# First product of expert slot 0 in the last dense block, a new order up to slot 5, and a shared copy of the last slot

## The chip, the cores and the metric

The kernel runs on one core of a Trainium2 chip. The metric is the device time of one execution in microseconds (us); lower is better. The core has engines that run side by side, each with its own queue of instructions taken in order: TensorE (PE; its weight loads are listed as PEld), VectorE (DVE), ScalarE (ACT), GpSimd (POOL) and SyncE (SP), which issues most DMAs. All times below are counted from the first instruction of the profiled execution, unless they are said to be counted from elsewhere.

## The reference

Three stages over 4608 tokens of width 512, cut to what is computed:

```python
# 1. attention in chunks of 64 tokens, 8 heads of 64
attn = softmax(q_c @ k_c.T / 8); out = attn @ v_c
# 2. dense layer, 512 -> 2048 -> 512
h = x @ w_in
g = max(h, 0) + alpha * min(h, 0)
x = g @ w_out
# 3. mixture of 8 experts, each token to its best one, 512 -> 1024 -> 512
logits = x @ w_gate;  expert = argmax(logits)
out[mask] = p[mask] * (max(x[mask] @ w1[e], 0) @ w2[e])   # p: softmax weight of the chosen expert
```

## The kernel before

**Stages.** Tokens are worked in 18 groups of 256, that is 36 tiles of 128 (`NTILE`). For each group attention gives x, and the dense layer takes 16 steps: step (j, m) makes 128 of the 2048 hidden columns (`mm1`, 12 products of 256 columns), and adds what they give to the group's output (`mm2`, 6 products of 512 columns, issued three steps later and interleaved with a later `mm1`). The written loop over steps 32 to 287 has two tables of extra work, `pre` and `bg`: what `at(step, f, ...)` puts there is issued in that step, `bg` behind the step's own `g_a`. The last block, steps 272 to 287, is group 17; `B0` is 272. All products are split in a high and a low part (hi and lo), so 4 slices of the contraction make 12 products.

**Gate and table.** When both tiles of a group are done, `gate_ev` copies a tile's rows out of PSUM on ScalarE, `gate_l` makes the 8 gate products on VectorE, `gate_a` and `gate_e` the choice and the exponential, `gate_r` ranks the tokens with two small products on TensorE (the second uses `ohsum`, the running count), and `gate_b` brings `ohsum` up to date on VectorE and scatters the rows into the expert-sorted buffer `xs` with an indirect DMA on GpSimd. After the last tile (35), `table_count`, `table_experts`, `table_places` and `table_base` compute on VectorE where each slot of 128 sorted rows begins (the register table `rt`).

**Slots.** Expert work goes in slots of 128 rows; 39 are always done here. `load(t)` brings a slot's rows. The first four slots (`FULL`) belong to the expert that has most tokens after group 16, known early; their loads need only that (`first`, `early_pick`). From slot 4 on `load` needs `rt`. `tx(t)` transposes the rows (`blocks`: transpose on VectorE into one of two z buffers, hi copy on ScalarE, lo on GpSimd). `m1(t, f)`, f = 0 or 1, is a first product (12 products of 512 columns) and 16 small copies with a Relu into `hx`, four for each 32-row part I; they run on ScalarE for f = 0 and for slots 0 to 2, otherwise on VectorE (line 728). `th(t, f)` transposes `hx` into `hT` by `blocks` again, `m2(t, f)` is a second product, and for f = 1 the scaling on ScalarE and the scatter to the output on GpSimd. So a slot is four groups of 12 products: (t, 0) and (t, 1) first, then `m2(t, 0)` and `m2(t, 1)`.

**Weights.** They lie split in HBM (`wsp`). The expert ring takes over the dense weights' memory: `load_early(x, c)` brings quarter c of the x-th early expert (2 MB) as soon as the dense layer has read the quarter under it for the last time: `load_early(0, 0..3)` at B0+4, 7, 12 and 15, `load_early(1, 0..3)` in the order below. `m1(t, f)` reads quarter f, `m2(t, f)` quarter 2 + f. Later experts come by `refill`.

**Order.** All is issued in the order in which it is written (`manual_schedule`), each engine takes its part in that order, and only data and buffers make it wait. After the last dense step come `mm2` of the last three steps and then the list `START` (line 920), which holds the last two tiles' gate, the table and the slots up to the second product of slot 4; then the loop of line 986 for the slots from 5 on, with slot t + 1's first products ahead of slot t's second ones.

Of the kernel before, what the change touches and what calls it, by code (L numbers as in the profile page):

```python
# [11 lines left out]
ACTF = mybir.ActivationFunctionType  # L12
ALU = mybir.AluOpType
# [24 lines left out]
def tile_attention_moe(ctx, tc, q, k, v, w_in, w_out, alpha, w_gate, w1, w2, out):  # L38
    nc = tc.nc
    NB = q.shape[0]  # L40
    NTILE = 2 * NB
    FULL = (NTILE - 4) // 8
    NT = 128 * NTILE
    MF = 16
    E = 8
# [57 lines left out]
    def bank(tag, name):  # L103
        return ps.tile([128, 512], F32, tag=tag, name=name)
# [3 lines left out]
    def pair(tag, name):  # L108
        return ps.tile([128, 2, 512], F32, tag=tag, name=name)

    def hbank(name, n=2):
        turn[0] = (turn[0] + 1) % n
        return bank(f"h{turn[0]}", name) if turn[0] < 2 else pair("s", name)[:, 0]
# [264 lines left out]
    def g_b(j, m):  # L378
        g_h(j, m)
        g_l(j, m)  # L380
# [62 lines left out]
        oh, se, lg = ohs[i]  # L443
        nc.scalar.activation(out=lg, in_=lg, func=ACTF.Exp, accum_out=se)

    rks = {}

    def gate_r(i):
        oh = ohs[i][0]
        if i < NTILE - 2:  # L450
            rk = pair("o", "rk")[:, 0, 0:E]
        else:
            rk = bank("y1", "rk")[:, 0:E]
        nc.tensor.matmul(out=rk, lhsT=tri, rhs=oh, start=True, stop=False)
        nc.tensor.matmul(out=rk, lhsT=ones, rhs=ohsum, start=False, stop=True)
        rks[i] = rk
# [114 lines left out]
    def at(step, f, *args):  # L571
        bg.setdefault(step, []).append((f, args))
# [45 lines left out]
    V = nc.vector  # L618
# [44 lines left out]
    xg, gi, xT, hx, hT, yp = {}, {}, {}, {}, {}, {}  # L663
# [32 lines left out]
    def blocks(dst, src):  # L696
        z = sg_u([128, 4, 4, 32], "z")
        V.transpose(out=z.rearrange("p b i r -> p i b r"), in_=src.rearrange("p i (b c) -> p i b c", b=4))  # L698
        z = z.rearrange("p b i r -> p b (i r)")
        nc.scalar.activation(out=dst[:, 0], in_=z, func=ACTF.Copy)  # L700
        nc.gpsimd.tensor_tensor(out=dst[:, 1], in0=z, in1=dst[:, 0].bitcast(F32), op=ALU.subtract)  # L701
# [5 lines left out]
    def passes(out, lhs, c, t, first, last):  # L707
        w = W2[c]
        rows_ = slice(0, 1) if t < FULL else bass.ds(half[t], 1)
        ins = []  # L710
        for a in range(4):
            for n, (xl, wl) in enumerate(((0, 0), (0, 1), (1, 0))):
                ins.append(nc.tensor.matmul(  # L713
                    out=out, lhsT=lhs[:, xl, a], rhs=w[:, rows_, wl, a],
                    start=(first and a == 0 and n == 0), stop=(last and a == 3 and n == 2),
                ))
        marks[t, c] = ins

    def m1(t, f):
        if f == 0 and t >= FULL:  # L720
            half[t] = nc.tensor.value_load(rt[0:1, 5, t:t + 1], min_val=0, max_val=1)
        p = hbank("h", 3)
        passes(p, xT[t], f, t, True, True)
        hx[t, f] = P2["hx"].tile([128, 4, 128], F32, name="hx")
        for I in range(4):
            for J in range(4):
                src, dst = p[32 * I:32 * I + 32, 128 * J:128 * J + 128], hx[t, f][32 * J:32 * J + 32, I]
                if f == 0 or t < FULL - 1:
                    nc.scalar.activation(out=dst, in_=src, func=ACTF.Relu)  # L729
                else:  # L730
                    V.tensor_scalar(out=dst, in0=src, scalar1=0.0, scalar2=None, op0=ALU.max)  # L731

    def th(t, f):
        if f == 0:
            hT[t] = xt_p.tile([128, 2, 2, 4, 128], F32R, tag="xt", name="hT")
        blocks(hT[t][:, f], hx.pop((t, f)))
# [29 lines left out]
        nc.gpsimd.memset(tbl([32, 5, 2, 32], "cols"), 0.0)  # L766

    def table_count():
        cps = pair("o", "cps")[:, 0, 0:E]
        nc.tensor.matmul(out=cps, lhsT=ones, rhs=ohsum, start=True, stop=False)  # L770
        nc.tensor.matmul(out=cps, lhsT=ones, rhs=ohs[NTILE - 1][0], start=False, stop=True)
        n = tbl([128, E], "n")
        V.tensor_tensor(out=n, in0=cps, in1=ebase, op=ALU.subtract)
# [137 lines left out]
    B0 = NS - MF  # L911
    at(B0 + 1, open_p2)
    for t in range(3):
        at(B0 + 2, load, t)
    at(B0 + 2, table_clear)
    at(B0 + 6, tx, 0)
    at(B0 + 6, load, 3)
    at(B0 + 9, tx, 1)
    a, b = NTILE - 2, NTILE - 1
    START = (  # L920
        (mm2, NB - 1, MF - 1), (gate_ev, a), (gate_l, a, 0, 4), (gate_ev, b), (gate_l, a, 4, 8), (gate_l, b, 0, 1),
        (gate_a, a), (m1, 0, 0), (m1, 0, 1), (th, 0, 0), (gate_e, a), (tx, 2), (gate_l, b, 1, 4), (gate_l, b, 4, 8),
        (m1, 1, 0), (load_early, 1, 0), (gate_r, a), (gate_b, a), (gate_a, b), (th, 0, 1), (m1, 1, 1), (tx, 3),
        (m2, 0, 0), (load_early, 1, 1), (gate_r, b), (th, 1, 0), (table_count,), (table_experts,), (gate_e, b),
        (m1, 2, 0), (gate_b, b), (th, 1, 1), (m2, 0, 1), (load_early, 1, 2), (table_places,), (m1, 2, 1),
        (load_early, 1, 3), (table_base,), (th, 2, 0), (table_next,), (th, 2, 1), (load, 4),
        (tx, 4), (m1, 3, 0), (table_refill,), (m2, 1, 0), (m1, 3, 1), (m2, 1, 1), (load, 5), (m2, 2, 0), (th, 3, 0),
        (tx, 5), (m2, 2, 1), (load, 6), (th, 3, 1), (m1, 4, 0), (m1, 4, 1), (tx, 6), (th, 4, 0),
        (m2, 3, 0), (th, 4, 1), (load, 7), (m1, 5, 0),
        (m2, 3, 1), (th, 5, 0), (m1, 5, 1), (refill, 4, 0), (load, 8), (m2, 4, 0), (th, 5, 1), (m2, 4, 1),  # L930
    )
    FIRST = 5

# [4 lines left out]
    with tc.manual_schedule():  # L938
        def warm(n):
            b = bank("h1", "warm")  # L940
            for _ in range(n):
                nc.tensor.matmul(out=b[:, 0:128], lhsT=ident, rhs=ident, start=True, stop=True)

        def by_step(f):
            return lambda x, *e: f(*order[x], *e)

        def hook(d):
            return lambda x: hooks(d, x)

        ops = dict(  # L950
            Q=load_part_qk, I=iload, G=lambda _: load_wgb(), V=load_v, N=lambda _: nc.sync.dma_start(out=calpha, in_=alpha), K=load_qk,
            Z=lambda _: consts(), W=warm, S=at_s, A=soft_a, B=soft_b, E=soft_e, C=soft_c, D=soft_d, T=at_pt, P=at_ptc, O=at_pv, H=at_xh, L=at_xl,
            v=conv_v, s=conv_s, u=conv_u, m=conv_m, h=conv_h, l=conv_l,
            X=by_step(mm1), Y=by_step(mm2), r=by_step(g_r), x=by_step(g_x), f=by_step(g_h), g=by_step(g_l),
            p=hook(pre), b=hook(bg),
        )
        engs = dict(V=nc.vector, G=nc.gpsimd)
        for t in ORDER.split():
            e = t[-1:]
            if e in engs:  # L960
                ops[t[0]](int(t[1:-1]), engs[e])
            else:
                ops[t[0]](int(t[1:]))
        done = 30
        for s in range(32, NS):
            j, m = order[s]
            hooks(pre, s)
            g_b(*order[s - 1])
            if done <= s - 3 and order[done][1]:
                mm1(j, m, mm2_parts(*order[done]))  # L970
                done += 1
            else:
                mm1(j, m)
            g_a(j, m)
            hooks(bg, s)
            while done <= s - 3:
                mm2(*order[done])
                done += 1
        hooks(pre, NS)
        hooks(bg, NS)  # L980
        g_b(j, m)
        mm2(j, m - 2)
        mm2(j, m - 1)
        for f, *args in START:
            f(*args)
        for t in range(FIRST, TS):
            more, two, dyn = t + 1 < TS, t + 2 < TS, t >= FULL
            if two: tx(t + 2)
            if more: m1(t + 1, 0)
            if more: m1(t + 1, 1)  # L990
            if dyn: refill(t, 0)
            if more:
                th(t + 1, 0)
                th(t + 1, 1)
            m2(t, 0)
            m2(t, 1)
            if t > FULL: refill(t - 1, 1)
            if t + 4 < TS: load(t + 4)
        refill(TS - 1, 1)
        n_s = nc.values_load(rt[0:1, 7, 0:1], min_val=NTILE, max_val=T)  # L1000
        with tc.If(n_s > TS):
            for t in range(TS, T):
                with tc.If(n_s > t):
                    load(t)
                    tx(t)
                    for f in range(2):
                        m1(t, f)
                    for f in range(2):
                        th(t, f)
                    for f in range(2):  # L1010
                        m2(t, f)
                    if t + 1 < T:
                        for c in range(2):
                            refill(t, c)
# [43 lines left out]
```

## Time and profile before

| | before |
|---|---|
| median of 3 runs | 1337.11 us (1336.64 to 1337.33) |
| profiled execution | 1337.11 us |
| its span, first to last instruction | 1335.3 us |
| PE busy | 1314.2 us, 98% |
| DVE busy | 971.0 us, 73% |
| ACT busy | 737.2 us, 55% |
| POOL busy | 694.7 us, 52% |
| mean granted TensorE clock | 0.995 of full |

Busy time is that of the engine's own instructions; waiting, and the issue of DMAs, is not counted. Ends of matmuls are modelled, and pipelined ones overlap, so the distance from one matmul's start to the next is the better measure of its cost. In a timeline a row is one or several like instructions in a row: start, time until the last one's end, engine, line, operation, tiles and shapes, count, and in brackets the idle time of the engine before it and what ended it. L12 is line 12 of the kernel. SPq and POOLq are the sequencers that issue DMAs.

### The profile page before, as it was taken

To read this page: it belongs to the slowest core of one execution; us is meant where nothing else is said; L and a number is where in the kernel's file an instruction comes from. 1 tells how busy PE (TensorE), PEld (TensorE's weight loads), DVE (VectorE), ACT (ScalarE), POOL (GpSimd) and SP (SyncE) were. 2 spreads that over 40 slices of the span, in tenths; PEclk is the share of its full clock that TensorE was granted. 3 is DMA by queue.
4 is the path that set the end of the run, shared out by engine and by line. 5 is a ranking of instruction groups with operands and counts; after the bars stand their busy time and mean duration, and the time that the engine had idled before them with its cause. 6 is when DMAs were issued, how large, how long until landed. Compare 5 with 4: busy or idle time off the path is not lost. (4 is left out here: it accounts for less than half of the span.)

```text
span 1335.3 us, 29880 instructions
## 1 busy us (share of the span) xinstructions
PE 1314.2 (98%) x9561; PEld 1146.6 (86%) x9561; DVE 971.0 (73%) x2483; ACT 737.2 (55%) x1961; POOL 694.7 (52%) x726
## 2 busy tenths in 40 slices
PE   8999999999999999999999999999999999999997
PEld 7898889888898888988889888887888888888885
DVE  7987887877877787887887786667766666656653
ACT  5654454555545556455555554338666666666663
POOL 3322346667676675766767664334444444444442
PEclk9999999999999999999999999998999999999999
DMA  9264415666666666566666661295224426866570
GB/s 364 82 202 148 106 49 180 221 201 202 218 208 209 209 213 222 196 225 204 199 221 204 208 213 64 62 338 208 62 59 174 174 62 260 320 248 229 191 272 35
DMA packets 107872, 249.07 MB, mean 187 GB/s; under 512 B 15104, under 2 KB 36096, under 8 KB 102592
## 3 DMA queue, kind: packets, MB, share of 16 engines
q1 hardware_dynamic: 101712, 227.37, 50.6%
q0 software_dynamic: 6000, 19.70, 4.0%
q8 instruction: 84, 1.38, 0.4%
q14 instruction: 76, 0.62, 0.2%
HBM read 401.39 MB, written 88.91 MB: 367 GB/s over the span
## 5 line engine op out<-in xcount | busy, mean ns | idle before, releaser
L342 PEld LDWEIGHTS h<-xt,ring 128*128 128x128 f32 x3456 | 610.3, 188 | 66.6 <-DVE xt L329 1.1
L342 PE MATMUL h<-xt,ring 128*128 128x256 f32 x3456 | 651.9, 282 | 1.0 <-DVE xt L329 0.9
L398 PE MATMUL y<-ring,g 128*128 128x512 f32 x1728 | 641.5, 395 | 0.3 <-POOL g L372 0.3
L372 POOL TENSOR_TENSOR g<-r,g 128x256 fp32r<-128x256 f32 x279 | 247.3, 888 | 189.1 <-ACT g L368 188.0
L398 PEld LDWEIGHTS y<-ring,g 128*128 128x128 f32 x1728 | 322.1, 188 | 10.9 <-POOL g L372 1.0
L423 DVE CUSTOM_DVE_ANT_0 junk<-row,wgb 128x512 bf16<-128x512 f32 x288 | 257.9, 895 | 7.4 <-ACT row L411 3.1
L359 ACT ACTIVATE r<-h 128x256 f32<-128x256 f32 x288 | 110.6, 384 | 263.7 <-PE h L342 214.3
L364 DVE SCALAR_TENSOR_TENSOR r<-r,calpha,h 128x256 f32<-128x256 f32 x288 | 137.1, 476 | 162.1 <-ACT r L359 162.0
L487 POOL TENSOR_TENSOR sp<-trio,sp 128x512 fp32r<-128x512 f32 x128 | 179.2, 1400 | 103.9 <-ACT sp L486 78.2
L731 DVE TENSOR_SCALAR hx<-h 32x128 f32<-32x128 f32 x576 | 165.3, 287 | 91.1 <-PE h L713 83.7
L713 PE MATMUL y<-ring,hT 128*128 (+1 forms) x936 | 221.7, 392 | 3.9 <-ACT hT L700 2.2
L713 PE MATMUL h<-ring,xT 128*128 (+1 forms) x936 | 219.7, 390 | 0.0
L701 POOL TENSOR_TENSOR hT<-z,hT 128x512 fp32r<-128x512 f32 x78 | 100.4, 1304 | 218.8 <-ACT hT L700 218.8
L713 PEld LDWEIGHTS y<-ring,hT 128*128 128x128 f32 x936 | 176.8, 189 | 42.2 <-ACT hT L700 3.1
L713 PEld LDWEIGHTS h<-ring,xT 128*128 128x128 f32 x936 | 176.1, 188 | 36.5
L729 ACT ACTIVATE hx<-h 32x128 f32<-32x128 f32 x672 | 179.5, 267 | 10.4 <-PE h L713 2.9
L368 ACT ACTIVATE g<-r 128x256 fp32r<-128x256 f32 x288 | 119.8, 416 | 79.8 <-DVE r L364 60.9
L700 ACT ACTIVATE hT<-z 128x512 fp32r<-128x512 f32 x78 | 48.0, 633 | 112.3 <-DVE z L698 112.1
L271 ACT ACTIVATE px<-s 32x256 f32<-32x256 f32 x240 | 89.7, 374 | 3.0 <-DVE s L260 0.2
L486 ACT ACTIVATE sp<-trio 128x512 fp32r<-128x512 f32 x128 | 80.4, 628 | 0.6
L698 DVE STREAM_TRANSPOSE z<-trio 128x512 f32<-128x512 f32 x39 | 27.6, 707 | 48.4 <-POOL hT L701 46.1
L701 POOL TENSOR_TENSOR xT<-z,xT 128x512 fp32r<-128x512 f32 x39 | 51.3, 1316 | 17.0 <-ACT xT L700 16.4
(167 smaller groups left out, 896.6 us busy)
## 6 DMA issues: line engine op xcount, KB each, us to landing
ring<-wsp SPq DMA_DIRECT2D x70, 4096.0 KB
wsp<-sp SPq DMA_DIRECT2D x128, 512.0 KB
trio<-in_w SPq DMA_DIRECT2D x128, 256.0 KB
ring<-wsp SPq DMA_DIRECT2D x8, 2048.0 KB
trio<-xs SPq DMA_DIRECT2D x156, 64.0 KB
vt<-in_v SPq DMA_DIRECT2D x18, 512.0 KB
qt<-in_q SPq DMA_DIRECT2D x17, 512.0 KB
kt<-in_k SPq DMA_DIRECT2D x17, 512.0 KB
```

The source lines that it names most:

```text
L342: nc.tensor.matmul(out=h, lhsT=w[:, wl, a, 128 * mi:128 * mi + 128], rhs=x[:, xl, a], start=(n == 0), stop=(n == 11),)
L359: nc.scalar.activation(out=r, in_=h, func=ACTF.Relu, scale=-1.0)
L364: nc.vector.scalar_tensor_tensor(out=r, in0=r, scalar=calpha[:, m:m + 1], in1=h, op0=ALU.mult, op1=ALU.add)
L368: nc.scalar.activation(out=gs[j, m][:, 0], in_=rs[j, m][0], func=ACTF.Copy)
L372: eng.tensor_tensor(out=g[:, 1], in0=r, in1=g[:, 0].bitcast(F32), op=ALU.subtract)
L398: nc.tensor.matmul(out=ys[j][t], lhsT=g[:, gl, 128 * t:128 * t + 128], rhs=w[:, wl, mi], start=(m == 0 and n == 0), stop=(m == MF - 1 and ...
L423: nc.vector.tensor_tensor_reduce(out=junk, in0=r[:, 0:512], in1=wgb[e // 2][:, e % 2], scale=1.0, scalar=0.0, op0=ALU.mult, op1=ALU.add, a ...
L487: eng.tensor_tensor(out=dst[:, 1], in0=raw, in1=dst[:, 0].bitcast(F32), op=ALU.subtract)
L701: nc.gpsimd.tensor_tensor(out=dst[:, 1], in0=z, in1=dst[:, 0].bitcast(F32), op=ALU.subtract)
L713: ins.append(nc.tensor.matmul(out=out, lhsT=lhs[:, xl, a], rhs=w[:, rows_, wl, a], start=(first and a == 0 and n == 0), stop=(last and a = ...
L729: nc.scalar.activation(out=dst, in_=src, func=ACTF.Relu)
L731: V.tensor_scalar(out=dst, in0=src, scalar1=0.0, scalar2=None, op0=ALU.max)
```

## The change

Four edits. The first product of slot 0 is split off its copies (`m1_mm`, `m1_relu`), and its two halves are issued in dense steps B0+8 and B0+9, into the pair of banks `s`; the 32 copies follow, four a step, in steps B0+9 to B0+15 (eight in the last), all on ScalarE. `th(0, 0)` goes to B0+13 and `tx(2)` to B0+14. The list `START` is rewritten. The rank of the last two tiles and the count use one pair of banks `o` instead of `y1` and another `o`. Slot 3's second half has its copies shared between VectorE and ScalarE, and so has the last slot (38), where the last quarter of the copies stands behind the first transpose.

```diff
     def gate_r(i):
         ...
-            rk = bank("y1", "rk")[:, 0:E]
+            if i == NTILE - 2:
+                last_rk.append(pair("o", "rk"))
+            rk = last_rk[0][:, i % 2, 0:E]
...
-    def m1(t, f):
+    hp, lead = {}, {}
+
+    def m1_mm(t, f):
         if f == 0 and t >= FULL:
             half[t] = nc.tensor.value_load(rt[0:1, 5, t:t + 1], min_val=0, max_val=1)
-        p = hbank("h", 3)
-        passes(p, xT[t], f, t, True, True)
+        hp[t, f] = (lead.setdefault(t, pair("s", "h")) if f == 0 else lead[t])[:, f] if t == 0 else hbank("h", 3)
+        passes(hp[t, f], xT[t], f, t, True, True)
         hx[t, f] = P2["hx"].tile([128, 4, 128], F32, name="hx")
+
+    def m1_relu(t, f, I, on_act):
+        p = hp[t, f]
+        for J in range(4):
+            src, dst = p[32 * I:32 * I + 32, 128 * J:128 * J + 128], hx[t, f][32 * J:32 * J + 32, I]
+            if on_act:
+                nc.scalar.activation(out=dst, in_=src, func=ACTF.Relu)
+            else:
+                V.tensor_scalar(out=dst, in0=src, scalar1=0.0, scalar2=None, op0=ALU.max)
+
+    def m1(t, f):
+        m1_mm(t, f)
         for I in range(4):
-            ...
+            m1_relu(t, f, I, f == 0 or t < FULL - 1)
...
     def table_count():
-        cps = pair("o", "cps")[:, 0, 0:E]
+        cps = last_rk[0][:, 1, E:2 * E]
...
     at(B0 + 6, tx, 0)
     at(B0 + 6, load, 3)
+    at(B0 + 8, m1_mm, 0, 0)
     at(B0 + 9, tx, 1)
+    at(B0 + 9, m1_mm, 0, 1)
+    for x, d in enumerate((9, 10, 11, 12, 13, 14, 15, 15)):
+        at(B0 + d, m1_relu, 0, x // 4, x % 4, True)
+    at(B0 + 13, th, 0, 0)
+    at(B0 + 14, tx, 2)
     a, b = NTILE - 2, NTILE - 1
     START = (
-        (mm2, NB - 1, MF - 1), (gate_ev, a), (gate_l, a, 0, 4), (gate_ev, b), (gate_l, a, 4, 8), (gate_l, b, 0, 1),
-        (gate_a, a), (m1, 0, 0), (m1, 0, 1), (th, 0, 0), (gate_e, a), (tx, 2), (gate_l, b, 1, 4), (gate_l, b, 4, 8),
-        (m1, 1, 0), (load_early, 1, 0), (gate_r, a), (gate_b, a), (gate_a, b), (th, 0, 1), (m1, 1, 1), (tx, 3),
-        (m2, 0, 0), (load_early, 1, 1), (gate_r, b), (th, 1, 0), (table_count,), (table_experts,), (gate_e, b),
-        (m1, 2, 0), (gate_b, b), (th, 1, 1), (m2, 0, 1), (load_early, 1, 2), (table_places,), (m1, 2, 1),
-        (load_early, 1, 3), (table_base,), (th, 2, 0), (table_next,), (th, 2, 1), (load, 4),
-        (tx, 4), (m1, 3, 0), (table_refill,), (m2, 1, 0), (m1, 3, 1), (m2, 1, 1), (load, 5), (m2, 2, 0), (th, 3, 0),
-        (tx, 5), (m2, 2, 1), (load, 6), (th, 3, 1), (m1, 4, 0), (m1, 4, 1), (tx, 6), (th, 4, 0),
-        (m2, 3, 0), (th, 4, 1), (load, 7), (m1, 5, 0),
-        (m2, 3, 1), (th, 5, 0), (m1, 5, 1), (refill, 4, 0), (load, 8), (m2, 4, 0), (th, 5, 1), (m2, 4, 1),
+        (th, 0, 1), (mm2, NB - 1, MF - 1), (load_early, 1, 0), (load_early, 1, 1), (load_early, 1, 2), (load_early, 1, 3),
+        (gate_ev, a), (gate_l, a, 0, 4), (gate_ev, b), (gate_l, a, 4, 8), (gate_a, a), (m1, 1, 0), (m1, 1, 1), (gate_e, a),
+        (m2, 0, 0), (th, 1, 0), (gate_l, b, 0, 4), (m2, 0, 1), (gate_r, a), (th, 1, 1), (m1, 2, 0), (tx, 3), (m2, 1, 0),
+        (gate_l, b, 4, 8), (gate_a, b), (gate_e, b), (gate_b, a), (th, 2, 0), (m1, 2, 1), (gate_r, b), (table_count,),
+        (m2, 1, 1), (table_experts,), (gate_b, b), (th, 2, 1), (m1, 3, 0), (table_places,), (m2, 2, 0), (table_base,),
+        (load, 4), (th, 3, 0), (m1_mm, 3, 1), (m1_relu, 3, 1, 0, False), (m1_relu, 3, 1, 1, False), (m1_relu, 3, 1, 2, True),
+        (m1_relu, 3, 1, 3, True), (m2, 2, 1), (tx, 4), (th, 3, 1), (load, 5), (m2, 3, 0), (m1, 4, 0), (table_next,),
+        (table_refill,), (tx, 5), (load, 6), (m2, 3, 1), (m1, 4, 1), (th, 4, 0), (m1, 5, 0), (tx, 6), (load, 7), (m2, 4, 0),
+        (th, 4, 1), (th, 5, 0), (m1, 5, 1), (refill, 4, 0), (load, 8), (th, 5, 1), (m2, 4, 1),
     )
...
             if two: tx(t + 2)
-            if more: m1(t + 1, 0)
-            if more: m1(t + 1, 1)
+            if two:
+                m1(t + 1, 0)
+                m1(t + 1, 1)
+            elif more:
+                m1(t + 1, 0)
+                m1_mm(t + 1, 1)
+                for I, on_act in ((0, False), (1, False), (2, True)):
+                    m1_relu(t + 1, 1, I, on_act)
             if dyn: refill(t, 0)
-            if more:
-                th(t + 1, 0)
-                th(t + 1, 1)
+            if more: th(t + 1, 0)
+            if more and not two: m1_relu(t + 1, 1, 3, False)
+            if more: th(t + 1, 1)
             m2(t, 0)
```

## Rows read from the trace of the kernel before

**Rows 1.** The page: the span, and busy time of each engine.

```profile
span 1335.3 us, 29880 instructions
...
PE 1314.2 (98%) x9561; PEld 1146.6 (86%) x9561; DVE 971.0 (73%) x2483; ACT 737.2 (55%) x1961; POOL 694.7 (52%) x726
```

**Rows 2.** Timeline of PE behind the last dense step.

```profile
889.34 3.65 PE L398 MATMUL y<-ring,g 128*128 128x512 f32 x14
...
902.53 2.98 PE L713 MATMUL h<-ring,xT 128*128 128x512 f32 x12
906.89 0.73 PE L713 MATMUL y<-ring,hT 128*128 128x512 f32 x2 [1.38 <-ACT hT L700]
908.65 4.63 PE L713 MATMUL y<-ring,hT 128*128 128x512 f32 x10 [1.03 <-POOL hT L701]
...
916.79 2.88 PE L713 MATMUL y<-ring,hT 128*128 128x512 f32 x12
...
954.89 5.60 PE L713 MATMUL y<-ring,hT 128*128 x24
960.33 0.84 PE L713 MATMUL h<-ring,xT 128*128 x3
```

**Rows 3.** Windows: length, PE, PEld, DVE, ACT, POOL busy, PEclk, DMA share, GB/s.

```profile
905.00:915.00 10.00, 7.59 (x24) 5.09 (x23) 8.02 (x26) 9.59 (x35) 5.68 (x4) 0.66 0.98 417
```

**Rows 4.** Timeline of the last slot.

```profile
1311.47 4.46 ACT L729 ACTIVATE hx<-h 32x128 f32<-32x128 f32 x16 [0.71 <-PE h L713]
...
1313.93 5.60 PE L713 MATMUL y<-ring,hT 128*128 x24
1314.12 4.80 DVE L731 TENSOR_SCALAR hx<-h 32x128 f32<-32x128 f32 x16 [4.75 <-PE h L713]
...
1320.38 0.73 PE L713 MATMUL y<-ring,hT 128*128 x2 [0.86 <-ACT hT L700]
...
1321.75 5.28 PE L713 MATMUL y<-ring,hT 128*128 x22 [0.63 <-POOL hT L701]
```

**Rows 5.** Timeline of SP, DVE and ACT in the last dense block.

```profile
864.51 0.37 SPq L652 DMA_DIRECT2D ring<-wsp  x1
...
866.10 0.71 DVE L698 STREAM_TRANSPOSE z<-trio 128x512 f32<-128x512 f32 x1
...
869.51 0.39 ACT L359 ACTIVATE r<-h 128x256 f32<-128x256 f32 x1 [0.43 <-PE h L342]
...
869.54 8.65 SPq L652 DMA_DIRECT2D ring<-wsp  x2
```

**Rows 6.** Windows of the transfers in the last dense block, columns as in rows 3.

```profile
864.50:874.00 9.50, 9.50 (x64) 8.64 (x63) 6.25 (x18) 2.81 (x7) 3.43 (x4) 1.00 0.94 296
874.00:878.00 4.00, 4.00 (x27) 3.61 (x26) 1.23 (x3) 1.91 (x7) 2.51 (x3) 1.00 0.93 393
...
885.00:886.40 1.40, 1.40 (x13) 1.15 (x11) 1.37 (x3) 0.21 (x2) 0.74 (x1) 1.00 0.06 23
```

**Rows 7.** Timeline of hi and lo copies behind a transpose, slot 36.

```profile
1297.94 1.23 ACT L700 ACTIVATE hT<-z 128x512 fp32r<-128x512 f32 x2 [3.10 <-DVE z L698]
1298.65 1.30 POOL L701 TENSOR_TENSOR hT<-z,hT 128x512 fp32r<-128x512 f32 x1 [5.84 <-ACT hT L700]
```

**Rows 8.** Timeline of DVE: gate of tile 34, count, table, slot 4's rows.

```profile
894.41 0.69 DVE L423 CUSTOM_DVE_ANT_0 junk<-row,wgb 128x512 bf16<-128x512 f32 x1 [3.11 <-ACT row L411]
...
901.01 0.15 DVE L432 TENSOR_REDUCE gmx<-lg 128x1 f32<-128x8 f32 x1
...
914.73 0.12 DVE L773 TENSOR_TENSOR n<-cps,ebase 128x8 f32<-128x8 f32 x1
...
927.07 0.18 DVE L858 TENSOR_SCALAR rt<-rt 1x64 int32<-1x64 int32 x1
...
931.82 0.71 DVE L698 STREAM_TRANSPOSE z<-trio 128x512 f32<-128x512 f32 x1 [2.27 <-DMA trio<-xs]
```

**Rows 9.** DMA issues of the whole span: count and median us to landing.

```profile
xs<-row,posi POOLq DMA_INDIRECT x36, 5.2
```

More of the change, by code (lines that the diff above doesn't have):

```diff
@@ L444, in gate_e @@
         nc.scalar.activation(out=lg, in_=lg, func=ACTF.Exp, accum_out=se)
-    rks = {}
+    rks, last_rk = {}, []
     def gate_r(i):
@@ L717, in passes @@
         marks[t, c] = ins
-    def m1(t, f):
+    hp, lead = {}, {}
+    def m1_mm(t, f):
         if f == 0 and t >= FULL:
             half[t] = nc.tensor.value_load(rt[0:1, 5, t:t + 1], min_val=0, max_val=1)
-        p = hbank("h", 3)
-        passes(p, xT[t], f, t, True, True)
+        hp[t, f] = (lead.setdefault(t, pair("s", "h")) if f == 0 else lead[t])[:, f] if t == 0 else hbank("h", 3)
+        passes(hp[t, f], xT[t], f, t, True, True)
         hx[t, f] = P2["hx"].tile([128, 4, 128], F32, name="hx")
-        for I in range(4):
[L726 to L731, printed above, removed]
+    def m1_relu(t, f, I, on_act):
[8 more added lines that the diff above has]
+        m1_mm(t, f)
+        for I in range(4):
+            m1_relu(t, f, I, f == 0 or t < FULL - 1)
     def th(t, f):
```

## The prediction

> **What bounds the kernel now.** I read the page first, then TensorE's own order around the change, then what its neighbours do there. The page: the span is 1335.3 us and TensorE is busy for 1314.2 us of it [rows 1]. The profiled execution took 1337.11 us, which is also the median of the three runs, so 1.8 us lie outside the span and every sum below is made against 1337.11. An engine that is busy for 98% gains nothing from less work elsewhere. The change adds and removes no product, so it can only shift TensorE's idle time and the stretches in which its clock is low.
>
> In TensorE's order [rows 2] a group of 12 expert products (one call) costs 2.72 us: 24 of them run from 954.89 to 960.33, 0.227 us each. Call T the moment 889.34, when the last first-product of the dense layer is done. The second product of slot 4 ends at 960.33, T+71.0. In between stand 18 dense products (4.1 us) and 22 groups (59.8 us), 63.9 in all. So 7.1 us are lost there, nearly all in one place: the group at 902.53 is done at 905.25, and then come two products at 906.89 (after ScalarE's hT), ten at 908.65 (after GpSimd's hT), and the group behind them. To 916.79 that is 11.54 us for 24 products (5.44), with 1.64 + 1.31 us idle. The other 3.1 us are the clock and four small products: the granted clock is 0.66 of full over the 10 us from 905 [rows 3], that is 6.8 us at the lower level, 1.2 GHz. The second place is the end [rows 4]: the group pair at 1313.93 is done at 1319.37, the last slot's second products start at 1320.38 and resume at 1321.75, 1.01 + 0.92 = 1.9 us idle. The reason stands beside them: 16 copies on VectorE (4.80 us) before either transpose.
>
> **First part: slot 0's first products in the dense block.** They stand at steps B0+8 and B0+9. Moving 24 products costs nothing by itself, 5.44 us before T instead of after. But TensorE takes its instructions in order, and everything of the dense layer is queued behind a product that waits. What it needs is xT of slot 0 and its weights. The transpose for xT starts at 866.10 (step B0+6); ScalarE's first read of h two steps later, at 869.51, marks the end of step B0+8 [rows 5]. xT is complete at 868.9 (transpose, then a hi copy of 0.63 and a lo of 1.30 us [rows 7]), in time. The weights are not: load_early(0, 0) is issued at 864.51 and load_early(0, 1) at 869.54, behind slot rows in SP's queue [rows 5], and the change moves neither. Each carries 2.1 MB. From 864.5 to 874.0 the transfers run at 296 GB/s, 2.04 MB by 871.4; to 878.0 it is 4.38 MB, and two weight loads and slot 3's rows are 4.46 MB, so the second cannot be there before 878.2. The third load is the second of the pair in rows 5 (877.84); nothing is issued behind it for 8.6 us, and its packets still move after 885 [rows 6], up to some 8.6 us after its issue. I take 8.6 to 9 us: the first at 873.4, the second at 878.5. TensorE arrives at 869.5, waits 3.9 us, runs 2.7 and the next dense step 2.8 (seven steps lie between 869.5 and T), and arrives for the second at 878.9: about 0.1. **Sum +4.0 us** (bounds 3.2 by bytes alone, 4.6).
>
> The Trainium skill, "DMA: Bandwidth & Descriptors", section "Anatomy of one DMA", gives per transfer about 2.0 us plus bytes at 436 GB/s (measured there on GpSimd's path), as an estimate 6.8 us for this load, hence 871.3 and 876.3. By it the wait would be 1.9 us and the whole forecast 2.1 us lower. The rows speak against it here, since the third load is under way for over 7.2 us.
>
> What hides work in the block: ScalarE's four copies a step (16 take 4.46 us, [rows 4]) are 1.1 us beside TensorE's 2.8 us step, with about 0.8 us of its own; costed at nothing. Only in the last step do eight of them (2.2 us) push the last dense g: +0.4 us, kept in the walk below.
>
> **The clock after that wait.** The trace has no 4 us wait in the dense block. Its nearest rows are those of 905: 2.95 us idle between 905.25 and 908.65, then 6.8 us at half clock in all, about 3 us lost. Bounds 0 and 3.4; I take **+2.5 us**.
>
> **Second part: the new order.** I walk it with the same durations, times from T: group 2.72, 16 copies on ScalarE 4.46, on VectorE 4.80 [rows 4], transpose 0.65 to the next instruction (0.71 in rows 5), hi copy 0.63 and lo 1.30 [rows 7]; eight gate products 5.9 (nine pieces from 894.41 to 901.01, 0.73 each), from the count to the table's rows 12.5 (914.73 to 927.2), from there to the transpose of slot 4's rows 4.6 [rows 8].
>
> Dense products end at 4.75 (0.65 of it idle, for the last g). Then TensorE runs (1,0), (1,1), both second products of slot 0 and (2,0) to 18.4 without a stop: hT(0) was made in the block. hT(1,0) is complete at 18.8, just in time. So the stall of 905 is gone. VectorE: gate of tile 34 to 12.3, transposes and gate of 35 with waits for copies (0.7) and for GpSimd's lo of slot 1 (1.6) to 23.4, gate_b(34) to 24.3; tile 35's rank waits for that, 0.5 us idle on TensorE. The count starts at 24.9, and with a wait for slot 2's copies the table's rows stand at 37.7. That is no earlier than before (37.9), while TensorE, with two groups less to do, is at slot 3's second product at 38.1. What is late next: the transpose of hT(3,0) is queued on VectorE behind the table: hi 39.0, lo 40.3, two idles of 0.9. Slot 4's rows are transposed at 42.3, hi 43.6, lo 44.9, TensorE at 42.6: 1.0 and 0.85 idle. (5,0) waits 0.75 for the lo of its rows.
>
> Then the worst place. (4,1) ends at 52.6. Its 16 copies stay on VectorE, and th(4,0) is queued behind them: transpose at 57.6, hi at 58.9, lo at 60.2. Between them TensorE has one group, (5,0); before it had four. It idles 2.8 and 0.85 us at m2(4,0). m2(4,1) waits 0.9 for its lo, and ends at 68.8. These are 20 groups and 18 products (58.5) and 10.3 us idle. With the two moved groups 74.2 against 71.0: **+3.2 us**. Bounds: only the idles that don't hang on the table (m2(4,0), m2(4,1)) leave 63.8, that is -1.8; a table 4 us later gives +7.
>
> At m2(4,0) TensorE is idle for 3.65 us, more than at 905, so the clock should fall again: 3.0, less the 0.9 of m2(4,1), which a slower TensorE no longer waits: **+2.0 us** (0 to 3).
>
> **Third part: last slot.** VectorE's eight copies end at 1316.5, ScalarE's quarter runs beside the transpose of hT(38,0), whose lo is ready at 1319.1 for 1319.4; the last quarter (1.2 us) and the second transpose give lo at 1321.0, needed at 1322.5. Both idles go: **-1.9 us** (bounds -1.9 and 0). The chain behind (scale, scatter) is unchanged.
>
> The banks for rank and count: same products, no wait beyond those walked.
>
> **Sum.** 4.0 + 2.5 + 3.2 + 2.0 - 1.9 = +9.8 us: 1346.9, say 1347.
>
> **Rivals.**
> Clock stays up in both new waits: +5.3, 1342.4. For it: the idles of 1 us at the end show no fall. Against it stands the fall of 905.
> Last scatter late: gate_b(35)'s scatter stands in GpSimd's queue behind slot 1's output, which waits for ScalarE until 30.6; issued at 31.7, median landing 5.2 us [rows 9], 36.9, while slot 4's load is wanted at 38.3. It decides from a landing of 6.6 us on; 3 us later and a third clock fall give 1350 to 1353.
> No wait for the weights: landing before 869.5. The bytes of the first part are against it. Then 3.2 + 2.0 - 1.9 = +3.3, 1340.4; with a table 2 us earlier, which takes as much from the idles at slots 3 and 4, 1338.4, no change that can be told.
> Faster: all other engines keep ahead of TensorE. The place is slots 3 to 5: with the table's rows by T+33 and the weights landed, only VectorE's copies of (4,1) stop TensorE: -1.8 - 1.9, 1333.4. For it: nearly all of the walk to 37 runs without a stop, and each of the terms against it is one row's duration in a long chain. Against: the count alone needs 12.5 us to its rows, and the weights' bytes.
>
> **How the numbers follow.** Forecast as summed 0.48 (own range 1343 to 1350), clock up 0.16, late scatter 0.10, small or no wait for weights 0.12, other engines ahead 0.14. This kernel's runs can't tell less than 0.2% (2.7 us) from no change, so faster is the last, 0.14; same (1334.4 to 1339.8) the one before, 0.12; slower 0.74. The range leaves out most of the faster case and the end of the late scatter: 1335 to 1353.
>
> **What would show it.** After: an idle TensorE of about 4 us ahead of the first expert product near 869.5, then a granted clock below 1 in the dense block; no wait between 905's counterpart and slot 2; waits for hT and xT copies at slots 3 and 4, the longest ahead of m2(4,0) behind VectorE's copies; no idle at the last slot. Wrong if the first expert product starts without a wait, or m2(4,0) follows (5,0) directly.

## The result, and the profile after

The changed kernel takes 1353.83 us (median of 5 runs, 1352.03 to 1357.53) against 1337.11 us before (5 runs, 1336.35 to 1339.14): a ratio of 1.0127, interval 1.0108 to 1.0145, or +16.7 us. Forecast were +9.8 us and a range that ended at 1353. The profiled execution is the longest of the five, 1357.53 us (mean granted clock 0.989, the other four 0.992 to 0.995), so the account of it below adds up to +20.4 us and not to +16.7.

The page of the changed kernel, span and busy time, answers to [rows 1]: 7.9 us more on PE and 20.5 us more span.

```profile
span 1355.8 us, 29874 instructions
...
PE 1322.1 (98%) x9561; PEld 1151.0 (85%) x9561; DVE 970.6 (72%) x2471; ACT 740.2 (55%) x1973; POOL 694.6 (51%) x726
```

PE's timeline in the changed kernel, the rows with a wait and those that mark its stretches (it answers to [rows 2]):

```profile
873.95 4.58 PE L715 MATMUL h<-ring,xT 128*128 128x512 f32 x12 [4.16 <-DMA ring<-wsp]
...
902.61 0.17 PE L456 MATMUL rk<-oh,tri 128*128 128x8 f16 x1 [1.55 <-DVE pos L476]
...
902.89 2.09 PE L398 MATMUL y<-ring,g 128*128 128x512 f32 x8
906.45 1.65 PE L398 MATMUL y<-ring,g 128*128 128x512 f32 x6 [1.46 <-POOL g L372]
...
909.40 5.61 PE L715 MATMUL h<-ring,xT 128*128 128x512 f32 x24
914.85 5.60 PE L715 MATMUL y<-ring,hT 128*128 128x512 f32 x24
...
930.93 0.17 PE L456 MATMUL rk<-oh,tri 128*128 128x8 f16 x1 [2.05 <-DVE pos L476]
...
951.48 0.73 PE L715 MATMUL h<-ring,xT 128*128 x2 [1.21 <-ACT xT L702]
953.55 4.63 PE L715 MATMUL h<-ring,xT 128*128 x10 [1.33 <-POOL xT L703]
...
970.74 6.00 PE L715 MATMUL y<-ring,hT 128*128 x12 [3.34 <-ACT hT L702]
...
979.41 2.88 PE L715 MATMUL y<-ring,hT 128*128 x12
```

T is 902.89 here. The group pair at 914.85 is slot 0's second product: what began at 906.89 before with two waits [rows 2] starts without one. But seven other places wait for over 1 us, and in four stretches the clock is low. Windows of the changed kernel, columns as in [rows 3]:

```profile
874.00:878.00 4.00, 4.00 (x11) 3.12 (x12) 0.00 (x0) 0.00 (x0) 0.00 (x0) 0.57 0.96 393
931.00:937.00 6.00, 5.91 (x22) 4.70 (x22) 5.04 (x28) 4.98 (x18) 2.27 (x2) 0.72 0.11 44
951.00:960.00 9.00, 7.19 (x18) 5.34 (x19) 6.82 (x24) 2.60 (x9) 3.53 (x3) 0.62 0.48 104
969.00:977.00 8.00, 6.12 (x14) 4.39 (x15) 2.29 (x4) 5.95 (x19) 2.51 (x2) 0.57 0.16 33
```

The granted clock falls to its lower level, 1.2 GHz, each time in or just behind one of the waits of 4.16, 2.05, 2.54 (1.21 + 1.33) and 3.34 us, and length times the missing clock gives 1.7, 1.7, 3.4 and 3.4 us lost: 1.7 in the dense block and 8.5 behind it. Before there was one such stretch behind T [rows 3], 3.4 us. Other traces have fewer such stretches; the section on the prediction comes back to this.

From these starts (slot 4's second product ends at 979.41 + 2.72) the +20.4 us of the profiled execution is laid out beside the forecast (us; "moved" is the 5.44 us of slot 0's first products, which now lie ahead of T):

| stretch | before | forecast | after | miss |
|---|---|---|---|---|
| T, less the moved products | 889.3 | +6.5 | 897.4 (+8.1) | +1.6 |
| T to the first product behind the dense layer | 4.9 | 4.75 | 6.5 | +1.75 |
| from there to slot 4's first product | 44.3 | 38.85 | 42.1 | +3.25 |
| from there to the end of slot 4's second product | 21.8 | 27.2 with the clock | 30.65 | +3.45 |
| all behind that | 376.8 | -1.9 | 375.4 (-1.4) | +0.5 |

The five misses make 10.6, the distance from +9.8 to +20.4. The five differences of after against before make +15.0, and with the 5.44 us of the moved products +20.4.

The last row is the tail; both waits of [rows 4] are gone. The last slot in the changed kernel:

```profile
1335.73 11.14 PE L715 MATMUL y<-ring,hT 128*128 x48
1335.93 2.36 DVE L737 TENSOR_SCALAR hx<-h 32x128 f32<-32x128 f32 x8 [4.75 <-PE h L715]
```

### Two things in it that the forecast had not

**ScalarE stands in the block.** ScalarE and VectorE in the last two dense steps of the changed kernel:

```profile
899.17 0.70 DVE L700 STREAM_TRANSPOSE z<-hx 128x512 f32<-128x512 f32 x1
...
899.90 0.63 ACT L702 ACTIVATE hT<-z 128x512 fp32r<-128x512 f32 x1 [3.40 <-DVE z L700]
900.44 0.40 ACT L368 ACTIVATE g<-r 128x256 fp32r<-128x256 f32 x1
900.75 0.36 ACT L359 ACTIVATE r<-h 128x256 f32<-128x256 f32 x1
...
901.15 0.48 DVE L364 SCALAR_TENSOR_TENSOR r<-r,calpha,h 128x256 f32<-128x256 f32 x1 [1.28 <-ACT r L359]
...
902.40 0.15 DVE L476 CUSTOM_DVE_ANT_0 rkt<-rk,oh 128x8 f32<-128x8 f32 x1
```

The hi copy of slot 0's transpose (`th(0, 0)`, step B0+13) is at the head of ScalarE's queue and waits 3.40 us, because its transpose is queued on VectorE behind the gate products of a tile of group 16. Behind it on ScalarE are the dense layer's own g (900.44) and its next r (900.75). VectorE's next instruction needs that r and stands idle for 1.28 us; the read of tile 32's rank (902.40) is queued behind it on VectorE, and TensorE's next rank, at 902.61, waits for that read. The rest of the block runs late behind it, up to the last g and the dense products at 906.45.

**VectorE is held beside GpSimd.** VectorE's and GpSimd's timelines between the gate of tile 35 and the table's rows (changed kernel; the two-input instructions of VectorE that took over 1 us, and what GpSimd ran then):

```profile
924.19 2.39 DVE L423 CUSTOM_DVE_ANT_0 junk<-row,wgb 128x512 bf16<-128x512 f32 x1
...
932.59 1.60 DVE L807 SCALAR_TENSOR_TENSOR cand<-n,oth 128x8 f32<-128x8 f32 x1
939.58 1.95 DVE L837 SCALAR_TENSOR_TENSOR pos<-lst,top,pos 128x8 f32<-128x8 f32 x1
```

```profile
924.72 1.30 POOL L703 TENSOR_TENSOR hT<-z,hT 128x512 fp32r<-128x512 f32 x1
...
932.87 1.29 POOL L703 TENSOR_TENSOR hT<-z,hT 128x512 fp32r<-128x512 f32 x1
...
940.20 1.30 POOL L703 TENSOR_TENSOR hT<-z,hT 128x512 fp32r<-128x512 f32 x1
```

A gate product takes 0.69 us in [rows 8] and 2.39 here; the other two forms take 0.16 and 0.23 in the table of the kernel before. The two of the table end at 934.19 and 941.53, 0.03 us behind GpSimd's lo copies (934.16 and 941.50), the gate product 0.56 us behind its copy (926.02). Together that is 1.70 + 1.44 + 1.72 = 4.9 us on the way to slot 4's rows; a fourth, in the choice for tile 35 (929.02, 0.94 us for 0.23), adds 0.7. No run takes GpSimd's copies away: that they are the cause is read from the ends. The Trainium skill, "SBUF — State Buffer", section "Who interferes with whom", says that VectorE and GpSimd share one pair of ports as an exclusive lock, so that one of them stands for the other's whole instruction; the ends agree with that. The page has the pair go to whichever starts first. VectorE's recorded start is 0.28 to 0.62 us ahead of the copy's each time, but GpSimd was by then in the instruction that issues an indirect DMA (from 923.67, 931.85 and 939.21, 1.0 us each) with the copy right behind it, so these rows don't decide that point.

The trace of before has such instructions on the same way, a gate product of tile 35 and one of the table:

```profile
907.52 1.63 DVE L423 CUSTOM_DVE_ANT_0 junk<-row,wgb 128x512 bf16<-128x512 f32 x1
...
923.81 1.28 DVE L852 SCALAR_TENSOR_TENSOR w<-w,ebase 32x16 f32<-32x16 f32 x1
```

### The profile page after: what moved, and what is told of

The parts are those of the page before. It is cut to its first block, busy times and chain, and to the rows that moved or that the text cites. A ratio compares the mean times of both kernels' runs of the same rounds, so it can differ in the third digit from the quotient of the medians.

```text
span 1355.8 us, 29874 instructions
## 1 busy us (share of the span) xinstructions
PE 1322.1 (98%) x9561; PEld 1151.0 (85%) x9561; DVE 970.6 (72%) x2471; ACT 740.2 (55%) x1973; POOL 694.6 (51%) x726
## 3 DMA queue, kind: packets, MB, share of 16 engines
q8 instruction: 84, 1.38, 0.4%
## 5 line engine op out<-in xcount | busy, mean ns | idle before, releaser
L737 DVE TENSOR_SCALAR hx<-h 32x128 f32<-32x128 f32 x564 | 161.8, 287 | 101.2 <-PE h L715 93.5
L715 PE MATMUL h<-ring,xT 128*128 (+1 forms) x936 | 224.0, 395 | 6.7 <-DMA ring<-wsp 4.2
L715 PE MATMUL y<-ring,hT 128*128 (+1 forms) x936 | 224.8, 396 | 4.0 <-ACT hT L702 3.3
L735 ACT ACTIVATE hx<-h 32x128 f32<-32x128 f32 x684 | 182.7, 267 | 19.4 <-PE h L715 9.5
L700 DVE STREAM_TRANSPOSE z<-trio 128x512 f32<-128x512 f32 x39 | 27.6, 709 | 49.1 <-POOL hT L703 47.5
```

The costliest lines, as they stand in the source:

```text
L715: ins.append(nc.tensor.matmul(out=out, lhsT=lhs[:, xl, a], rhs=w[:, rows_, wl, a], start=(first and a == 0 and n == 0), stop=(last and a = ...
```

## The experiments

Before ran at 1337.1 to 1337.5 us beside all of them; differences "to after" are to 1353.83. The interval of after is 5 us wide, so of the trials that undo one part only the weights (just) and the joint one are told from it by time alone; the others are read by their traces.

**The block alone, old order (e6).** Slot 0's products, copies and `th(0, 0)` in the dense block; the order of before without these three.

```diff
+    at(B0 + 8, m1_mm, 0, 0)
     at(B0 + 9, tx, 1)
+    at(B0 + 9, m1_mm, 0, 1)
+    ... copies and th(0, 0) as in the change
-        (gate_a, a), (m1, 0, 0), (m1, 0, 1), (th, 0, 0), (gate_e, a), ...
+        (gate_a, a), (gate_e, a), ...
```

> The kernel before with one part of the change alone: slot 0's first products, their copies and th(0,0) in the last dense block; the old order otherwise, without these three. Theory (waits in TensorE's order: 4.2 us for the weights, 1.7 us of low clock behind it, 3.3 us because th(0,0) holds up ScalarE's dense copies): the block costs about 8 to 9 us, and the stall of 905 (6 us) goes, some 2 us of it coming back as waits for the table: 1340 to 1344 us, with no wait ahead of the second products of slot 0. Rival (the whole loss is made in the block, the new order costs nothing): about 1353 us.

1349.07 us (ratio 1.0089, 1.0072 to 1.0105), 5 us over what I expected. T is 901.46, so the block alone costs 12.1 - 5.44 = 6.7 us. That is close to the forecast's 4.0 + 2.5, but by luck: in this trace it is 3.4 for the weights, 1.7 for the clock and 1.4 for waits at tile 33's rank. The surprise is behind T: slot 4's first product comes 45.8 us behind it (947.22), 49.2 before, so of the 5.44 us taken out of this stretch 2.0 are spent again. By the end of slot 4's second product (971.53 here) it is T+70.1 against T+71.0: all but 0.9 is spent, although the low clock behind T cost 1.7 us here and 3.4 before. The old order had slot 0's products as the work that covers tile 34's gate; without them PE waits there:

```profile
872.68 4.57 PE L713 MATMUL h<-ring,xT 128*128 128x512 f32 x12 [3.39 <-DMA ring<-wsp]
...
914.44 0.19 PE L454 MATMUL rk<-oh,tri 128*128 128x8 f16 x1 [4.79 <-DVE oh L437]
...
971.53 5.60 PE L713 MATMUL h<-ring,xT 128*128 x24
```

After, with the tail's edit as well, is 4.8 us slower than this trial (the intervals 1.0072 to 1.0105 and 1.0108 to 1.0145 don't overlap): the new order itself costs time. In e6 the table's rows stand at T+37.0, in after at T+42.1.

**The weights first (e2).** After, with the first weights ahead of slot rows in SP's queue.

```diff
-    for t in range(3):
-        at(B0 + 2, load, t)
+    at(B0 + 2, load, 0)
+    at(B0 + 4, load, 1)
+    at(B0 + 4, load, 2)
...
-    at(B0 + 6, load, 3)
+    at(B0 + 7, load, 3)
```

> The changed kernel with load_early(0,0) issued ahead of the rows of slots 1 and 2, and load_early(0,1) ahead of slot 3's rows; nothing else. Theory (the wait of 4.2 us is for the weights and for them alone, and the low clock behind it is its child): no wait ahead of the first expert product, full clock there, 1347 to 1349 us. Rival (the transfers are bound by bytes, so what is moved ahead delays what is behind, and the wait only turns up at the second one): over 1351 us, with a wait at step B0+9.

1349.88 us (1.0091, 1.0074 to 1.0108), 3.95 under after and 0.9 over what the theory had. The first load is now issued at 857.03 instead of 865.09. The first product starts without a wait at full clock, and a part of the rival's wait comes at the second:

```profile
869.53 2.89 PE L715 MATMUL h<-ring,xT 128*128 128x512 f32 x12
...
876.41 3.06 PE L715 MATMUL h<-ring,xT 128*128 128x512 f32 x12 [1.17 <-DMA ring<-wsp]
```

**The wait filled (e7).** After, with 16 products that nothing reads (32 in the row below) ahead of slot 0's first: PE is busy while the weights come.

```diff
+    at(B0 + 8, fill_wait, 16)
     at(B0 + 8, m1_mm, 0, 0)
```

> The changed kernel with 16 products of no use (some 3.7 us of TensorE, into a bank that nobody reads) ahead of slot 0's first product, so that TensorE works while the weights come. Theory (a wait costs its own length, the clock behind it about 1.7 us): the clock stays full in the block, the wait shrinks to about 0.5 us, 1351 to 1353 us. Rival (most of the loss is the clock, the waits themselves are covered): 1348 us or less.

1351.47 us (1.0111, 1.0094 to 1.0127), 2.4 under after, though slot 0's product still starts 3.8 us behind the dense work ahead of it (4.2 in after):

```profile
868.89 3.73 PE L932 MATMUL fill<-ident 128*128 128x128 f32 x32
872.72 3.01 PE L715 MATMUL h<-ring,xT 128*128 128x512 f32 x12
```

The 12 products then take 3.01 us instead of 4.58: the clock after an idle PE is a cost of its own beside the wait, 1.6 us by these two rows. The two intervals overlap, so the 2.4 us is no more than in line with the 2.5 forecast.

**Slot 0's transpose behind the block (e4).**

```diff
-    at(B0 + 13, th, 0, 0)
-    at(B0 + 14, tx, 2)
...
-        (th, 0, 1), (mm2, NB - 1, MF - 1), ...
+        (th, 0, 0), (mm2, NB - 1, MF - 1), (th, 0, 1), (tx, 2), ...
```

> The changed kernel with th(0,0) and tx(2) moved from the dense block to the head of the list behind it. Theory (in the block ScalarE waits 3.4 us for th(0,0)'s transpose, which VectorE does behind tile 33's gate, and the dense g stands behind that wait): the waits of 1.55 us for the rank and 1.5 us for g go, 1350 to 1351 us. Rival (the 32 copies crowd ScalarE in the block): the waits stay, about 1353.5 us.

1350.38 us (1.0107, 1.0088 to 1.0126), 3.45 under after. The wait of 902.61 (1.55 us) is gone, and of the one at 906.45 (1.73 with the row behind it) 0.77 + 0.15 are left, so the trace bears out 2.4 us of it:

```profile
902.49 0.73 PE L398 MATMUL y<-ring,g 128*128 128x512 f32 x2 [0.77 <-ACT g L368]
903.38 1.19 PE L398 MATMUL y<-ring,g 128*128 128x512 f32 x4 [0.15 <-POOL g L372]
```

**The transpose of (4,0) ahead of the copies of (4,1) (e5).**

```diff
-        (m1, 4, 1), (th, 4, 0), (m1, 5, 0)
+        (m1_mm, 4, 1), (th, 4, 0), (m1_relu, 4, 1, 0, False), ..., (m1_relu, 4, 1, 3, False), (m1, 5, 0)
```

> The changed kernel with th(4,0) ahead of the 16 copies of (4,1) on VectorE. Theory (m2(4,0) waits because its transpose is queued behind those copies): that wait (2.5 to 3.3 us) and the low clock behind it go, some 2 us come back at m2(4,1), whose own copies end as late as before: 1349 to 1351 us. Rival (VectorE's time in this stretch is the limit, whatever stands first): the wait turns up whole at m2(4,1), 1353 us or more.

1350.6 us (1.0101, 1.0086 to 1.0117), 3.2 under after. The wait of 3.34 us is gone and so is the low clock behind it; half of the wait comes back one product later:

```profile
964.15 2.89 PE L715 MATMUL y<-ring,hT 128*128 x12
...
970.12 0.73 PE L715 MATMUL y<-ring,hT 128*128 x2 [0.36 <-ACT hT L702]
972.21 2.58 PE L715 MATMUL y<-ring,hT 128*128 x10 [1.36 <-POOL hT L703]
```

**All three at once (e8)**, that is the edits of e2, e4 and e5 together.

> The changed kernel with three mends together: weights ahead of the slots' rows, th(0,0) and tx(2) behind the block, th(4,0) ahead of the copies of (4,1). Theory (the mends add up, what is left are the waits for the rank of tile 35 and for the table's rows, for which 14 groups behind the dense layer are too few): 1341 to 1345 us, still over before, with the waits ahead of the rank and at slots 3 and 4. Rival (without these three the change gains what it removes at 905): 1335 us or less.

1344.59 us (1.0051, 1.0035 to 1.0066): 9.2 under after, 10.6 by the sum of the three, and still 7 over before. What is left is a wait for the second weights in the block, and behind T the waits at tile 35's rank and at slot 4's rows:

```profile
876.55 3.02 PE L715 MATMUL h<-ring,xT 128*128 128x512 f32 x12 [2.11 <-DMA ring<-wsp]
...
923.99 0.17 PE L456 MATMUL rk<-oh,tri 128*128 128x8 f16 x1 [2.17 <-DVE pos L476]
...
944.56 0.73 PE L715 MATMUL h<-ring,xT 128*128 x2 [1.20 <-ACT xT L702]
946.62 4.12 PE L715 MATMUL h<-ring,xT 128*128 x10 [1.33 <-POOL xT L703]
```

**More work on VectorE's way to the table, after (e12) and before (e13).** Four gate products of tile 35 made twice in either kernel.

```diff
-        (gate_l, b, 4, 8), ...
+        (gate_l, b, 4, 8), (gate_l, b, 4, 8), ...
```

> The changed kernel with four gate products of tile 35 made twice (2.9 us more on VectorE ahead of the rank, the table and slot 4's rows; the values are the same). Theory: behind the dense layer TensorE already waits for this way over VectorE (2.05 us at tile 35's rank, 2.5 us at slot 4's rows), so nearly all of the 2.9 us comes through: 2.5 to 4.5 us more than the changed kernel's 1353.8, some of it by the clock. Rival: the waits there are those of single copies, which have room elsewhere: 0 to 1 us more.

> The kernel before with the same four gate products of tile 35 made twice, 2.9 us more on VectorE at the same place of the way. Theory: here slot 0's products stand behind the dense layer and TensorE's stall at its second product leaves VectorE time: its rank of tile 35 at 913.09 has waited for nothing (one-hot ready at 911.1), so about 1 us of the 2.9 shows there and nothing later: 1337.1 to 1338.5. Rival: the way over VectorE sets the end of this part before too: 1339.5 to 1341.

After takes all of the 2.9 us and more by the medians: 1358.19 us (1.0157, 1.0144 to 1.0171), +4.4, or +4.0 by the two ratios, whose intervals just touch. Before takes 1339.46 us (1.0014, 1.0005 to 1.0023), +1.9: over the range of my theory and at the lower edge of the rival's. By the times alone the two effects can't be told apart. The rank of tile 35 and then slot 4's first product, of e12; the rank and the end of slot 4's second product, of e13:

```profile
933.02 0.17 PE L456 MATMUL rk<-oh,tri 128*128 128x8 f16 x1 [5.27 <-DVE pos L476]
...
953.58 0.73 PE L715 MATMUL h<-ring,xT 128*128 x2 [1.17 <-ACT xT L702]
```

```profile
914.07 0.17 PE L454 MATMUL rk<-oh,tri 128*128 128x8 f16 x1 [1.88 <-DVE oh L437]
...
962.79 5.60 PE L713 MATMUL h<-ring,xT 128*128 x24
```

The start of slot 4's first product is counted from T. With the new order it is T+48.6 in after, 48.6, 48.1, 48.7, 48.6 and 48.1 in e2, e4, e5, e7 and e8, although 13 groups of products and what is left of the dense layer need only about 40 us; and T+51.8 in e12 (T is 901.78 there), 3.2 later. It is the same whether the clock fell at tile 35's rank (after, e4, e7) or not (e2, e5, e8). So with this order the stretch is as long as VectorE's way, whatever is mended ahead of T. In the order of before it is T+49.2 with 14 groups, and T+49.9 in e13. That 0.7 is too small a figure for the 2.9 us, since the low clock behind T cost 3.4 us in the profile of before and 1.7 in e13's. The end of slot 4's second product stands at T+74.0 in e13 and at T+71.0 before: by then all of the 2.9 us shows. So the rival held, and VectorE's work on this way comes through to TensorE in both orders.

**The tail alone (e1, e10).** In the first trial my edit had also put slot 0's two halves into one pair of banks, as the changed kernel does; the second left its banks alone.

```diff
-            if more: m1(t + 1, 0)
-            if more: m1(t + 1, 1)
+            ... the last slot's shared copies, as in the change
```

> The kernel before with the shared copies of the last slot alone. Theory (both idles ahead of the last second products are VectorE's 16 copies): no idle there, 1.9 us less, 1335.2 us on the median of before. Rival (the end is set by the output scatter, not by TensorE): the same time as before.

1340.29 us (1.0019, 1.001 to 1.0028), slower than before. The tail's waits are gone, but PE stands at the first products:

```profile
901.85 7.27 PE L713 MATMUL h<-ring,xT 128*128 128x512 f32 x24 [4.55 <-ACT hx L733]
```

With copies issued between them, the second half of a pair that counts as one tile waited for the readers of the first. So this trial says nothing of the tail.

> The kernel before with the last slot's shared copies alone; the new functions m1_mm and m1_relu are there, and slot 0 keeps its banks of before (which the earlier trial of the tail did not). Theory: of the two idles at the last slot, 1.0 and 0.9 us, both go and nothing else moves: 1.9 us less than before, 1335.3 to 1335.6. Rival: the end is set by something else (the last scatter), so no change: 1337.2. Rival 2: the split of the copies over two engines delays the transposes: over 1337.5.

1336.35 us (0.9992, 0.9983 to 1.0001), 0.8 under before by the medians, not told from no change; its profiled execution (1335.14) is 1.97 shorter than the one before, and the last slot's products follow without a stop:

```profile
1313.96 11.15 PE L713 MATMUL y<-ring,hT 128*128 x48
```

**Another order with slot 0 behind the dense layer (e9, e11).** The plain tail, and an order of my own: slot 0's transpose between the copies of its two halves, copies of slots 1 to 3 divided. In e11 tile 35's rank and the count come one group later, the copies of (2,1) on ScalarE, the rest of the table behind slot 4's transposes.

```diff
-        (gate_a, a), (m1, 0, 0), (m1, 0, 1), (th, 0, 0), ...
+        (gate_a, a), (m1, 0, 0), (m1_mm, 0, 1), (R, 0, 1, True, 0), (th, 0, 0), (tx, 2), (R, 0, 1, True, 1, 2, 3), ...
```

> The kernel before with slot 0's first products left behind the dense layer, the shared copies of the last slot, and another order behind the dense layer: th(0,0) stands inside the copies of (0,1), the rank of tile 35 behind (2,0), second products as early as their copies allow, half the copies of (2,1) on VectorE. Theory (the stall of 905 is the place of th(0,0) in ScalarE's queue, and 16 groups behind the dense layer cover the table's chain): no wait of over 1 us up to slot 4, 1330 to 1333 us. Rival (the stall only moves on to the table's rows, as in the changed kernel): 1335 us or more, with waits at slots 3 and 4.

1340.33 us (1.0024, 1.0015 to 1.0033): the stall of 905 is gone, and new waits take its place:

```profile
911.91 0.17 PE L454 MATMUL rk<-oh,tri 128*128 128x8 f16 x1 [2.06 <-DVE oh L437]
```

The other large ones are in front of two second products (1.38 + 0.65 us at 934.32, 1.49 + 1.33 at 956.11).

> My own order (slot 0's products behind the dense layer) mended at the places where its trace showed waits: tile 35's rank and the count one group of products later, the copies of (2,1) on ScalarE around the transpose of (2,0), the rest of the table behind slot 4's transposes; the plain tail stays. Theory that each wait was that one instruction's place in a queue: its 2.06, 2.03 and 2.82 us and the two stretches of low clock behind them (1.7 and 3.4) go, less about 1 us at the second product of (0,1), whose lo copy is ready 1 us late: from 1340.3 to 1331 to 1334, under both kernels. Rival: the way from the gate of tile 35 over the table to slot 4's rows sets the end of this part whatever TensorE's order, so that the idle time only moves to slots 3 and 4: 1336 to 1340.

1336.6 us (0.9996, 0.9987 to 1.0005), no change that can be told from before, with the tail's edit in it: by its time the rival held, though slot 4's first product itself waits for nothing here. No low clock is left behind T, but that product stands at T+50.0, as in e9 (T+49.9) and little later than before; the idle time lies spread over six places, the longest of them

```profile
917.67 3.01 PE L713 MATMUL y<-ring,hT 128*128 128x512 f32 x12 [1.63 <-DVE pos L474]
```

No version beat the kernel before by more than can be measured.

## Why the prediction was right in direction and wrong in size

**The weights: right.** "TensorE arrives at 869.5, waits 3.9 us": it waited 4.16 us, with the weights 8.9 us behind the load's issue, at 865.09 (forecast 8.6 to 9). The second product came without a wait. In e4, e5, e6 and e12, which leave the loads alone, the same wait was 3.0 to 3.6 us, so 4.16 is the long end of it. The 6.8 us that the formula of the Trainium skill, "DMA: Bandwidth & Descriptors", section "Anatomy of one DMA", gave would have meant 1.9 us of wait; the measurement decides against it for this load. e2 takes the wait away by the load's place in the queue alone.

**The clock after it: right in kind.** Forecast 2.5; the windows show 1.7.

**"What hides work in the block ... costed at nothing": the step that failed first.** I summed ScalarE's busy time against a step and asked whether it fits. It fits; what I left out is that `th(0, 0)` in the block makes ScalarE wait for VectorE, with the dense layer's g and r behind the waiting copy. 1.55 us of the first line of the account and 0.8 of the 1.75 of its second line are this, the 2.4 us that e4 takes away; the 0.9 that e4 leaves stands with the eight copies of the last step still in the block, for which the walk had +0.4.

**The new order: the walk was right in its places, its VectorE too fast.** Slots 0 to 2 run without the stall, the rows of slot 4 and `m2(4,0)` wait where the walk had them (1.2 + 1.3 against 1.0 + 0.85; 3.34 against 2.8). But "the table's rows stand at 37.7" was T+42.1 (944.99), and tile 35's rank waited 2.05 instead of 0.5. Of these 4.4 us 1.3 were there when tile 34's gate was done (916.45, T+13.6 for 12.3), behind the late dense products. Another 2.9 came up to the end of tile 35's gate (930.46, T+27.6 for 23.4), 2.4 of them in two held instructions, since the walk had each gate product at its undisturbed 0.69. From the count to the rows it was only 0.5 longer (13.3 for 12.8) with 3.2 us held in it, because the 12.5 us of [rows 8] had a held instruction (923.81) and an idle 1.00 in them already. With it goes my bound "only the idles that don't hang on the table leave 63.8": e8 and e12 show that the table's way sets this stretch with the new order. The two moved groups had run beside a way through VectorE that didn't get shorter without them: slot 4's first product began 49.2 us behind T before and begins 48.6 us behind it now, so most of the 5.44 us that lie ahead of T were simply added. The new order has a part in that, since e6 with the old one had the table's rows at T+37.0 and this product at T+45.8; but it too had gained only 0.9 us by the end of slot 4's second product.

**The clock at m2(4,0): too few falls.** Forecast was one fall behind T, +2.0; there were three, 8.5 us in the profiled execution. The other four runs have a mean clock 0.003 to 0.006 higher and are 2.7 to 5.5 us shorter. The traces of e2, e4 and e7, which leave `m2(4,0)` as it is, have two falls behind T of 1.7 us each, one at `m2(4,0)` and one ahead of it. So how many waits are followed by a fall differs from run to run; the size of the one forecast was about right, and one fall was fewer than any of these traces has.

**The tail: right in place.** -1.9 forecast; -1.4 in the profile of after, -1.97 between the profiled executions of e10 and before, but -0.8 by their medians (-2.3 to +0.1).

Of the rivals, "last scatter late" gave nearly the right time, but isn't what happened: the scatter was issued at 939.21 and landed at most 3.9 us later in this trace, ahead of the table's rows at 944.99, and it is for the table that SyncE waited with slot 4's load. What the runs don't settle is how the 16.7 us of the median split, since the median run was not the profiled one. With two falls as in e2, e4 and e7 (3.4 us for 8.5) the account would come to some 15.3 us, an estimate.

## What to carry to other kernels

Before work is put into a stage that runs full, look on each engine's queue for who is behind it when its input is late: an engine with half its time free still stops the stage if the head of its queue waits. Work taken out of a stretch saves time only if that work was what the stretch was waiting on; find the longest way through the other engines first, by doubling a piece of it as e12 and e13 do. And in a walk over VectorE, count the instructions that will stand beside GpSimd's at what they take there.

## What the runs showed of the hardware that I had not expected

A VectorE instruction of 0.16 to 0.69 us can last 1.6 to 2.8 us when GpSimd runs a two-input instruction in it; the trace of before has it too (1.63 and 1.28 us), and the walk left it out. The clearest case in the changed kernel, a 32x2 operation and two of GpSimd's lo copies one behind the other, VectorE and then GpSimd:

```profile
951.91 2.83 DVE L885 TENSOR_SCALAR has<-ordt,mo 32x2 f32<-32x2 f32 x1
```

```profile
952.19 1.30 POOL L703 TENSOR_TENSOR xT<-z,xT 128x512 fp32r<-128x512 f32 x1
953.41 1.30 POOL L703 TENSOR_TENSOR hT<-z,hT 128x512 fp32r<-128x512 f32 x1
```

The first ends at 954.74, 0.03 us behind the second copy: by these ends an instruction can be held over two of the other engine's in a row. And a wait of 2 us was enough for the granted clock to fall behind it, but not each time: at tile 35's rank it fell behind 2.05, 2.17 and 2.06 us in after, e4 and e7 and stayed full behind 2.06, 2.05 and 2.17 us in e2, e5 and e8. The length of a wait alone didn't decide.
